# A new hand-written order of 1,343 operations in a fused hash-attention and channel-mix kernel

## The chip, the cores and the metric

The kernel runs on one core of one Trainium2 chip. The metric is the device time of one launch in microseconds; three runs of the kernel before gave a median of 245.75 us (245.43 to 245.88). Five engines work beside each other, each through its own instruction stream in order: PE (matrix multiplications), DVE (VectorE), ACT (ScalarE), POOL (GpSimd) and SP, which here only issues DMA transfers.

## The reference

Two stages are computed. The first is attention in which a query sees only the keys of its own hash bucket: six random projections give six sign bits for each query and key, and scores between different buckets are masked out before the softmax. The second is a channel mix over the attention's output.

```python
q_bits = (np.einsum('bhsd,dk->bhsk', q, proj) > 0).astype(np.int64)
k_bits = (np.einsum('bhsd,dk->bhsk', k, proj) > 0).astype(np.int64)
...
mask = q_bucket[:, :, :, None] == k_bucket[:, :, None, :]
scores = scale * np.matmul(q, k.transpose(0, 1, 3, 2))
scores = np.where(mask, scores, -1000000000.0)
...
attn = attn / (np.sum(attn, axis=-1, keepdims=True) + 1e-09)
return np.matmul(attn, v).astype(np.float32)
...
xk = mu_k * x + (1.0 - mu_k) * x_prev
xr = mu_r * x + (1.0 - mu_r) * x_prev
k = np.maximum(xk @ w_k, 0.0)
v = k * k @ w_v
r = 1.0 / (1.0 + np.exp(-(xr @ w_r)))
return (r * v).astype(np.float32)
```

The sizes are 4 batches, 8 heads, 768 positions and 64 values per head; the channel mix has width 512 and an inner width of 1,024. Inputs and output are float32.

## The kernel before

Two heads of one batch make a pair; there are 16 pairs, numbered 0 to 15, and four of them make a batch. For pair n the operations are, by the names that the code gives them:

- `ldq`, `ldv` (lines 360 and 365): loads of q, k and v, issued by SP. `wl` are loads of the weights.
- `hi`, `lo` (lines 265 and 431, on DVE from pair 2 on): q and k split into two 16-bit halves, high and low. `tr` (line 435): a DMA transpose of the split tensor into the tile `a`, issued by SP. Pairs 2 and 3 do this for q and k apart, later pairs in one piece. Pairs 0 and 1 are transposed on PE, with copies `evt` out of PSUM (line 259).
- `bits` (line 455, PE): the six projections; `bx` (line 458, DVE): their signs out of PSUM; `row` (line 259, POOL or DVE): four copies of the signs into rows of `a`, one for each of q and k of each head (`row1q1` is pair 1, q, second head). With those rows a matching bucket adds a large number to the score, which is how the mask is made.
- `sc` n_0 to n_8 (line 633, PE): the scores in nine steps of 1,024 columns; `exp` (line 637, ACT): their exponentials into the tile `pt`.
- `oo` n_0 and n_1 (line 660, PE): scores times v, three pieces for each head; `rc` and `ob` (lines 671 to 678, DVE): division by the row sums.
- `ot` with `xt`, or `otd` (lines 688, 694): the output transposed, on PE or by a DMA; `xs`, `df`, `xk`, `xr` (lines 701 to 733, DVE): the shifted mix, the inputs of the second stage.
- `va`, `mc` (lines 410 and 417, DVE) with `mean` (PE) and `vsum` (POOL): v less its mean.

After each fourth pair come the operations of the channel mix of that batch: `kp` (line 748, PE) with `relu` (line 754, ACT) and `sq` (line 759, DVE), `r` (line 772, PE) with `tanh` (line 775, ACT), and `v` (line 785, PE) with `os` (line 792, DVE) and the store `st` (line 795). They are spread among the attention of later pairs.

Nothing of this is ordered by the place in the source. Each `plan.add` only appends an operation to a list, with its reads and writes. The list `ORDER` then says in which order the operations are emitted, and each engine runs its own operations in that order. `BANKS` says which PSUM bank each result takes, or for `sc` and `bits` which pair of banks; a result that takes a bank waits until the operation that frees the bank's last content has run. `ENGS` says on which engine an operation runs where there is a choice. The waits between engines are put in from what is read and written, so every order that respects the data is correct; but an engine that has come to an operation whose input isn't there stands, with all that is behind it.

The score buffers `a` are 4 deep, `nat` (loads of q and k) 3, `nh` (the split) 2, `pt` 2.

Of the kernel before, what the change touches and what calls it, by code (L numbers as in the profile page):

```python
# [103 lines left out]
class Plan:  # L104
# [10 lines left out]
    def add(self, eng, dur, fn, r=(), w=(), take=None, give=(), name="", at=0.0, svc=0.0, tr=0, port=0, alts=()):  # L115
        o = Op()
        o.alts = alts
        if alts:
            e = ENGS[self.flex] if ENGS else eng
            self.flex += 1  # L120
            fn = lambda f=fn, e=e: f(e)
# [748 lines left out]
```

## Time and profile before

| | us |
|---|---|
| median of three runs | 245.75 |
| the profiled execution | 245.72 |
| its span, first to last instruction | 243.7 |
| PE busy, 2,466 matmuls | 231.5 |
| DVE busy, 407 instructions | 195.0 |
| ACT busy, 247 instructions | 185.2 |
| POOL busy, 140 instructions | 90.5 |

The span is 2.0 us shorter than the time of the execution it was taken from. In the timelines a row gives the start of a stretch of like instructions, its length, the engine and line, what it writes and reads, how many instructions it holds, and in brackets the idle time of the engine ahead of it with what ended it. In the windows a row gives, for a stretch of time, its length and the busy time and instructions of PE, of PE's weight loads, of DVE, ACT and POOL, then the granted clock of PE, the share of the DMA engines and the rate.

### The profile page before, as it was taken

Reading aid. Unit: us, or ns where it says so; the run is one execution under the profiler, and the core shown is the slowest. Engines: PE = TensorE matmul, PEld = TensorE weight load, DVE = VectorE, ACT = ScalarE, POOL = GpSimd, SP = SyncE. Lnnn points to the kernel's source line nnn. Section 1 sums busy time; section 2 is a strip of 40 time slices with the busy share of each in tenths; the row PEclk is TensorE's granted clock in tenths of the full one; section 3 lists DMA queues with packets and bytes.
Section 4 is the critical chain, followed back from the end, with each engine's and each line's share of the span. In section 5 each row is a group of like instructions: output and inputs, shape, how many; then the busy total and the mean of one; then the engine's idle time right before and its main releaser. Section 6 shows DMA issues by size and latency. Waiting matters only on the chain.

```text
span 243.7 us, 6161 instructions
## 1 busy us (share of the span) xinstructions
PE 231.5 (95%) x2466; PEld 143.1 (59%) x2486; DVE 195.0 (80%) x407; ACT 185.2 (76%) x247; POOL 90.5 (37%) x140
## 2 busy tenths in 40 slices
PE   8998899998989999999999999999999999999994
PEld 6654566675656656565658565556565764555443
DVE  3998899999999999899989999956556779636342
ACT  3999999998988889888889948898987860145420
POOL 5691756797755966505225260105020000000000
PEclk9999999999999999999999999999999999999999
DMA  6989999999999899999999929149302030222033
GB/s 227 377 238 194 216 238 212 310 222 377 280 241 225 287 236 258 233 255 240 261 222 251 181 62 175 54 107 208 118 3 58 9 116 5 87 86 89 0 129 129
DMA packets 72523, 43.97 MB, mean 180 GB/s; under 512 B 54832, under 2 KB 67504, under 8 KB 72496
## 3 DMA queue, kind: packets, MB, share of 16 engines
q1 hardware_dynamic: 72272, 43.40, 73.2%
q8 instruction: 19, 0.31, 0.5%
q10 hardware_dynamic: 224, 0.20, 0.2%
q14 instruction: 8, 0.07, 0.1%
HBM read 24.12 MB, written 6.29 MB: 125 GB/s over the span
## 4 chain that ended last, share of the span: by engine, by line
PE 60%; DVE 23%; DMA 7%; ACT 4%; issue 4%; SPq 1%; DVEq 0%; ACTq 0%
PE ps_all L785 17%; PE ps_all L633 12%; PE ps_all L748 11%; PE ps_all L772 8%; PE ps_all L660 7%; DMA a<-nh 5%; DVE nh L431 4%; DVE nh L265 3%; DVE k L759 3%; ACT pt L637 3%; DVE bx L458 3%; DVE a L259 2%; PE ps_all L455 2%; DMA mur<-in_moe_mu_r_dram 2%; PE ps_all L282 2%
## 5 line engine op out<-in xcount | busy, mean ns | idle before, releaser
L637 ACT ACTIVATE pt<-ps_all 128x1024 bf16<-128x1024 f32 x144 | 139.7, 1043 | 13.4 <-PE ps_all L633 12.0
L633 PE MATMUL ps_all<-a 128*128 128x512 f16 (+1 forms) x384 | 81.2, 325 | 3.0 <-ACT pt L637 0.9
L259 POOL COPY a<-bx 6x384 f32<-6x384 f32 x46 | 34.8, 756 | 54.3 <-DVE bx L458 18.1
L660 PEld LDWEIGHTS <-pt 128*128 128x128 bf16 x1152 | 43.9, 97 | 10.7 <-issue 1.1
L748 PE MATMUL ps_all<-xk,wk 128*128 128x384 bf16 x256 | 48.6, 326 | 1.1 <-DVE ob L678 1.1
L633 PEld LDWEIGHTS <-a 128*128 128x128 f16 x384 | 33.3, 97 | 25.6 <-issue 5.3
L660 PE MATMUL ps_all<-va,pt 128*128 128x65 bf16 x1152 | 46.4, 193 | 0.0
L785 PE MATMUL ps_all<-wv,k 128*128 128x512 bf16 (+2 forms) x200 | 45.3, 362 | 0.3
L754 ACT ACTIVATE kr<-ps_all 128x384 bf16<-128x384 f32 x64 | 29.7, 507 | 20.9 <-PE ps_all L748 16.2
L759 DVE TENSOR_TENSOR k<-kr 128x384 bf16<-128x384 bf16 x64 | 25.0, 414 | 13.5 <-ACT kr L754 13.1
L748 PEld LDWEIGHTS <-wk 128*128 128x128 bf16 x256 | 24.0, 98 | 17.0 <-issue 1.7
L785 PEld LDWEIGHTS <-k 128*128 128x128 bf16 x208 | 19.5, 98 | 19.4
L431 DVE SCALAR_TENSOR_TENSOR nh<-nat,nh 128x1536 f16<-128x1536 f32 (+1 forms) x16 | 27.9, 1744 | 0.2
L792 DVE SCALAR_TENSOR_TENSOR os<-rs,ps_all 128x512 f32<-128x512 f32 (+2 forms) x26 | 16.6, 643 | 13.2 <-PE ps_all L785 8.8
L775 ACT ACTIVATE rs<-ps_all 128x512 f32<-128x512 f32 x24 | 14.3, 600 | 15.0 <-DVE os L792 8.5
L772 PE MATMUL ps_all<-wr,xr 128*128 128x512 bf16 x84 | 23.3, 379 | 0.8 <-issue 0.2
L386 POOL TENSOR_TENSOR vt<-vn 128x384 f32<-128x384 f32 x12 | 13.8, 1148 | 20.0 <-DMA vn<-in_v_dram 19.6
L678 DVE TENSOR_TENSOR ob<-ps_all,rc 128x384 bf16<-128x384 f32 x32 | 17.7, 554 | 0.7
L265 DVE TENSOR_SCALAR nh<-nat 128x1536 f16<-128x1536 f32 (+2 forms) x21 | 16.8, 809 | 0.7 <-DMA nat<-in_k_dram 0.5
L458 DVE TENSOR_SCALAR bx<-ps_all 128x768 uint16<-128x768 uint16 x15 | 14.2, 954 | 2.8 <-ACT pt L637 2.3
L410 DVE SCALAR_TENSOR_TENSOR va<-ps_all,vn 128x384 bf16<-128x384 f32 x24 | 12.7, 548 | 2.9 <-PE ps_all L405 2.9
L772 PEld LDWEIGHTS <-xr 128*128 128x128 bf16 x96 | 9.0, 97 | 9.4 <-issue 0.5
(94 smaller groups left out, 190.1 us busy)
## 6 DMA issues: line engine op xcount, KB each, us to landing
vn<-in_v_dram SPq DMA_DIRECT2D x16, 384.0 KB, 4.9
out_dram<-os SPq DMA_DIRECT2D x23, 256.0 KB, 2.3
nat<-in_q_dram SPq DMA_DIRECT2D x15, 384.0 KB, 5.2
nat<-in_k_dram SPq DMA_DIRECT2D x15, 384.0 KB, 5.7
wst<-in_moe_w_k_dram SPq DMA_DIRECT2D x2, 512.0 KB, 7.7
wst<-in_moe_w_r_dram SPq DMA_DIRECT2D x2, 512.0 KB, 7.6
wst<-in_moe_w_v_dram SPq DMA_DIRECT2D x2, 512.0 KB, 6.2
k<-in_moe_w_k_dram SPq DMA_DIRECT2D x1, 512.0 KB, 6.5
```

Source lines behind the costliest of these rows:

```text
L259: nc.scalar.copy(o, i_) if e == "ACT" else tt_on(e).tensor_copy(o, i_)
L265: tt_on(e).tensor_scalar(out=o, in0=i_, scalar1=QS, scalar2=None, op0=ALU.mult)
L431: nc.vector.scalar_tensor_tensor(out=nh[:, :, D:P], in0=nat.rearrange("p j (c d) -> p (j c) d", d=D), scalar=QS, in1=nh[:, :, 0:D], op0=AL ...
L458: nc.vector.tensor_scalar(out=bx_t[sx][0:rows].bitcast(U16), in0=ps_t[plan.slot[nm]][0:rows, 0:S].bitcast(U16).rearrange("p (c e) -> p c e ...
L633: nc.tensor.matmul(ps[:, lo - s * STEP : hi - s * STEP], side_a["k"][sa][:, j, jc * P : (jc + 1) * P], side_a["q"][sa][:, j, q0 : q0 + hi ...
L637: nc.scalar.activation(out=pt_t[sp][:, s * STEP : (s + 1) * STEP], in_=ps_t[plan.slot[nm]], func=AF.Exp, bias=EBIAS, scale=ESC)
L660: nc.tensor.matmul(oo[:, ic * 65 : ic * 65 + 65], pt_t[sp][:, o : o + P], va_t[sa][:, j, jc, 0 : D + 1], start=(not uc and ic == 0 and jc ...
L748: nc.tensor.matmul(ps[:, 0:HALF], wk_sb[:, d, fc * P : (fc + 1) * P], xk_t[mx[d]][:, h * HALF : (h + 1) * HALF], start=(d == 0), stop=(d = ...
L754: nc.scalar.activation(out=kr_t[sk], in_=i_, func=AF.Relu, scale=0.5 ** 0.5)
L759: nc.vector.tensor_tensor(out=k2_t[s2][:, h * HALF : (h + 1) * HALF], in0=kr_t[sk], in1=kr_t[sk], op=ALU.mult)
L772: nc.tensor.matmul(sm(nr), xr_t[mx[d]][:, c * P : (c + 1) * P], wr_sb[:, d, :], start=(d == 0), stop=(d == NDC - 1))
L785: nc.tensor.matmul(sm(nv)[:, x0:x1], k2_t[(b * NFC + fc) % NK2][:, c * P : (c + 1) * P], wv_sb[:, fc, x0:x1], start=(fc == 0), stop=(fc == ...
```

## The change

`ORDER` and `BANKS` are replaced; `ENGS` and every operation stay. Of the operations on each engine, counted by their place in that engine's own sequence, these have another one than before: PE 366 of 466 (the first at its 48th), DVE 312 of 383 (from its 26th), ACT 182 of 247 (from its 27th), POOL 76 of 133 (from its 35th), SP none of 114. 225 of the 337 names of PSUM results are in another bank. In `Plan.add`, three lines are added, which put the duration and port of the chosen engine into the plan's record.

```diff
-    73, 78, 1, 75, 26, 27, 33, 34, 35, 30, 31, 76, 74, 79, 28, 29, 32, 40, 118, 77, 119, 80, 120, 41, 42, 43, 44, 45, 46, 47, 48, 84, 85,
...
-    139, 189, 190, 117, 140, 49, 23, 24, 153, 148, 25, 149, 191, 192, 152, 154, 141, 155, 142, 159, 150, 241, 157, 144, 143, 193, 160, 146,
-    165, 163, 156, 242, 158, 145, 166, 164, 161, 167, 168, 169, 244, 245, 216, 217, 204, 205, 235, 210, 212, 243, 246, 194, 162, 195, 211,
...
+    73, 1, 27, 33, 34, 35, 0, 2, 3, 4, 5, 6, 7, 8, 9, 10, 37, 36, 38, 39, 78, 76, 74, 75, 82, 83, 125, 79, 118, 77, 133, 126, 111, 119, 30,
...
+    154, 25, 191, 140, 149, 141, 155, 159, 192, 241, 142, 146, 242, 244, 144, 150, 160, 156, 157, 158, 165, 166, 163, 164, 216, 161, 245,
+    143, 145, 204, 217, 205, 162, 190, 49, 193, 235, 243, 194, 246, 288, 287, 51, 183, 170, 50, 212, 167, 294, 208, 195, 213, 171, 210, 295,
...
         if alts:
             e = ENGS[self.flex] if ENGS else eng
             self.flex += 1
+            for a in alts:
+                if a[0] == e and e != eng: dur, port = a[1], a[2]
+            eng = e
             fn = lambda f=fn, e=e: f(e)
```

Read by names (the number in `ORDER` in brackets), these stretches of single engines are those that the prediction speaks of. The first is DVE from its 23rd operation on:

```
before: evt1k0(132) evt1q1(136) lo2(189) evt1k1(140) hi2(191) lo2(192) bx1(142) hi3(241) row1q1(144) row1q0(143) row1k1(146)
        lo3(242) row1k0(145) rc0(168) ob0(169) hi3(244) lo3(245) bx2(195)
after:  evt1k0(132) evt1q1(136) lo2(189) hi2(191) evt1k1(140) lo2(192) hi3(241) bx1(142) row1k1(146) lo3(242) hi3(244)
        row1q1(144) lo3(245) row1q0(143) row1k0(145) muk(50) hi4(294) bx2(195)
```

PE, from its 42nd, and POOL, from its 35th:

```
PE before:   sc0_1 bits1 sc0_4 sc0_6 sc0_5 oo0_0 sc0_8 oo0_0 sc0_7 oo0_0 sc1_8 sc1_2 sc1_5 sc1_6 bits2 sc1_4
PE after:    sc0_1 bits1 sc0_4 sc0_6 sc0_5 oo0_0 oo0_0 sc0_8 sc1_8 sc0_7 sc1_2 bits2 oo0_1 sc1_6 oo0_0 sc1_4
POOL before: va2 vsum2 vsum2b row2k0 row2q0 row2k1 row2q1 vsum2c row3k1 row3q1 row3k0 row3q0
POOL after:  row2q1 row2q0 row2k0 va2 row2k1 vsum2 vsum2b row3q1 row3k0 row3k1 row3q0 vsum2c
```

On ACT `exp1_8 exp1_2 exp0_7` follow each other before and after. Next, DVE from its 49th and PE around `bits4`:

```
DVE before: lo5 va3 rc1 ob1 rc1 ob1 muk xs0 bx4 df0 xr0 xt1 hi6 xk0 lo6 rc2 rc2 ob2 xs1 ob2 bx5
DVE after:  mur lo5 xs0 va3 df0 xr0 rc1 ob1 rc1 ob1 bx4 hi6 xt1 lo6 rc2 rc2 xs1 ob2 ob2 df1 bx5
PE before:  oo1_1 sc2_5 bits4 sc3_0 sc3_3 sc3_6 ot1 sc3_5 oo2_0 sc2_8
PE after:   oo1_0 sc2_5 sc3_8 sc3_0 bits4 sc3_3 oo2_0 sc3_5 oo2_0 ot1
```

After the change `sc3_0` takes the two banks that the two `ob1` free. Further on, `bits6` stands ahead of `sc5_7` before and behind it after. Last, DVE from about its 101st and PE around `bits7`:

```
DVE before: sq0_2 hi8 sq0_3 lo8 rc5 ob5 sq0_2 sq0_4 sq0_3 xr2 sq0_6 bx7
DVE after:  sq0_1 hi8 xz5 xr3 sq0_2 lo8 bx7 rc5 sq0_3 ob5
PE before:  sc6_8 kp0_6_0 sc6_5 bits7 kp0_5_1 kp0_6_0 sc6_1
PE after:   sc6_8 bits7 kp0_3_1 kp0_6_0 sc6_5 kp0_4_1 oo5_0 sc6_1
```

There `kp0_5_1` takes the bank that the first `ob5` frees before the change, and `sc6_1` takes the banks that `bx7` frees after it. Up to `sc6_1`, PE has run the same operations in both but for these: the kernel before has eight more `kp` matmuls ahead of it (both parts of `kp0_4_0`, the first of `kp0_5_1`, the last of `kp0_6_0`), the kernel after three `kp` matmuls (the first part of `kp0_4_1`) and twelve of `oo5_0`.

114 rows, old and new, of tables (BANKS, ORDER) are left out of this document.

## The prediction

> **What bounds the kernel now.** I read the page first, then windows of 10 us, then who waited for whom, then timelines of single engines.
>
> ```profile
> span 243.7 us, 6161 instructions
> ...
> PE   8998899998989999999999999999999999999994
> ...
> DVE  3998899999999999899989999956556779636342
> ...
> DMA  6989999999999899999999929149302030222033
> ```
>
> ```profile
> 20.00:30.00 10.00, 8.16 (x101) 4.60 (x98) 8.41 (x13) 9.62 (x11) 4.41 (x5) 1.00 0.91 207
> 30.00:40.00 10.00, 9.65 (x141) 6.52 (x139) 9.47 (x16) 10.00 (x12) 5.91 (x10) 1.00 1.18 250
> 40.00:50.00 10.00, 9.57 (x170) 6.76 (x167) 9.93 (x16) 9.72 (x11) 7.68 (x10) 1.00 0.99 270
> 50.00:60.00 10.00, 9.05 (x142) 6.31 (x141) 9.67 (x18) 9.07 (x11) 8.57 (x8) 1.00 1.12 285
> 60.00:70.00 10.00, 10.00 (x104) 6.55 (x103) 9.42 (x17) 10.00 (x17) 8.52 (x10) 1.00 1.12 261
> 70.00:80.00 10.00, 8.90 (x107) 5.72 (x106) 9.59 (x22) 8.02 (x13) 4.26 (x7) 1.00 1.26 228
> 80.00:90.00 10.00, 9.62 (x114) 5.77 (x115) 9.90 (x19) 8.41 (x12) 7.61 (x7) 1.00 1.18 317
> 140.00:150.00 10.00, 9.44 (x120) 6.07 (x114) 9.76 (x23) 6.80 (x10) 4.09 (x4) 1.00 0.56 118
> ```
>
> The granted clock (the column after POOL's) is 1.00 throughout, so the time is PE's work plus the holes in it. PE works without a break in the second half; its holes lie in these eight windows and sum to 1.84 + 0.35 + 0.43 + 0.95 + 0.00 + 1.10 + 0.38 + 0.56 = 5.6 us. That is all a new order can win after 20 us. In the same windows up to 90 us DVE is busy 9.4 to 9.9 of 10 us from 30 us on and ACT nearly as much, so a hole of PE is there mostly the shadow of a full DVE or ACT, or of a transfer:
>
> ```profile
> PEld L455 <- DMA a<-nh: 2.4, 4, 1.0
> ...
> PE ps_all L748 <- DVE ob L678: 1.1, 1, 1.1
> ```
>
> **The change part by part.** The three lines in Plan.add touch a record that schedule doesn't read, and SP's order stays: both cost nothing. The rest is order. I follow the places where an operation now stands behind another.
>
> First stretch, from 14.6 us:
>
> ```profile
> 15.07 0.74 DVE L265 TENSOR_SCALAR nh<-nat 128x768 f16<-128x768 f32 x1
> ...
> 18.39 1.76 DVE L259 COPY a<-bx 6x384 f32<-6x384 f32 x3
> 20.18 0.96 DVE L431 SCALAR_TENSOR_TENSOR nh<-nat,nh 128x768 f16<-128x768 f32 x1
> 21.17 0.35 DVE L259 COPY a<-bx 6x384 f32<-6x384 f32 x1
> ...
> 22.25 0.55 DVE L265 TENSOR_SCALAR nh<-nat 128x768 f16<-128x768 f32 x1
> 22.84 0.96 DVE L431 SCALAR_TENSOR_TENSOR nh<-nat,nh 128x768 f16<-128x768 f32 x1
> ```
>
> ```profile
> 21.57 1.48 PE L633 MATMUL ps_all<-a 128*128 128x256 f16 x9 [0.76 <-DVE a L259]
> ```
>
> ```profile
> 22.22 23.96 ACT L637 ACTIVATE pt<-ps_all 128x1024 bf16<-128x1024 f32 x26 [0.35 <-PE ps_all L633]
> 46.35 10.41 ACT L637 ACTIVATE pt<-ps_all 128x1024 bf16<-128x1024 f32 x11 [0.17 <-PE ps_all L633]
> 57.69 4.69 ACT L637 ACTIVATE pt<-ps_all 128x1024 bf16<-128x1024 f32 x5 [0.93 <-PE ps_all L633]
> ```
>
> ```profile
> L259 DVE COPY a<-bx x14: 351/362/894, 18.4 to 183.3; 6x384 f32<-6x384 f32 x14
> ```
>
> ```profile
> 18.03 1.05 POOL L386 TENSOR_TENSOR vt<-va 128x390 f32<-128x390 bf16 x1
> ```
>
> hi2 now runs ahead of evt1k1, which bits1 waits for: that is up to 0.74 us on bits1, sc0_4 and sc0_6 and the exponentials behind them. It does not add to what follows, since the next wait of ACT ends later. sc1_2 waits for row1k0, the copy at 21.17, and PE (hole of 0.76) and ACT (0.35) stood for it already. In the new order a second hi3 and lo3 (0.55 + 0.96) run ahead of it, so it ends 1.51 us later. From this comes off what the copies gain: the dearest of the 14 took 0.894, the median 0.362, and the three at 18.39 sum to 1.76; while they ran, POOL ran vsum2 (the 1.05 row), which now stands behind the row copies of pair 2. If row1q1 falls to the median, 0.53 comes off. So exp1_2 starts between 0.98 and 1.51 us later; I take 1.0, since POOL has nothing to run there. exp0_7 stands behind exp1_2 and cannot fill the gap. ACT then goes without a break for 23.96 us, 26 exponentials of 0.92 each, so this 1.0 is kept until its next hole.
>
> On the shared port, the Trainium skill (SBUF — State Buffer, Who interferes with whom) says that a VectorE instruction in a two-port mode and a GpSimd instruction block each other for a whole instruction, whoever issues first. By that rule the copy falls to 0.36 and the delay is 0.98; by the row alone, if 0.89 is what a first copy costs, it is 1.51. The trace agrees as far as it goes: the dear copy is the one that ran beside POOL.
>
> The same move makes both lo3 earlier. Ahead of the first, two of the three copies go (1.76 less one of 0.36, so 1.4 us); the second then follows it by one hi3 and one copy, and starts at 20.7 to 21.2 in place of 22.84. With them go the transposes of pair 3, whose first SP issued right after lo3 (20.18 + 0.96):
>
> ```profile
> 21.16 4.09 SPq L435 DMA_TRANSPOSE a<-nh  x2
> ```
>
> ```profile
> 44.94 0.83 PE L455 MATMUL ps_all<-a,p 128*32 128x512 f16 x16 [0.43 <-DMA a<-nh]
> ```
>
> The DMA engines are full from there (share 0.91 to 1.26), so whatever is queued behind, the transposes of pairs 4 to 6 too, may land 1.4 to 2 us earlier. What this can win is the 2.4 us in which PE waited for a transpose, at bits5 for one (the second row), and ACT's holes of 0.17 and 0.93. I count none of it in the sum: ACT's 1.0 us at 22 us takes up ACT's two holes, and the next stretch takes the transposes off PE's path.
>
> POOL: va2, vsum2 and vsum2b (0.8 to 1.05 each) move from a hole of POOL to behind row copies. Their first reader is oo2_0, which PE reaches after bits4 in both orders (36.32 before); that hides them.
>
> Second stretch:
>
> ```profile
> 36.50 0.56 DVE L678 TENSOR_TENSOR ob<-ps_all,rc 128x384 bf16<-128x384 f32 x1
> ...
> 37.30 0.96 DVE L458 TENSOR_SCALAR bx<-ps_all 128x768 uint16<-128x768 uint16 x1
> ...
> 38.76 1.14 DVE L724 SCALAR_TENSOR_TENSOR xr<-df,mur,xt 128x768 bf16<-128x768 bf16 x1
> ```
>
> ```profile
> 36.32 0.83 PE L455 MATMUL ps_all<-a,p 128*32 128x512 f16 x16
> 37.14 0.59 PE L633 MATMUL ps_all<-a 128*128 128x512 f16 x3
> ```
>
> Before, bits4 ran while DVE did ob1, and bx4 followed ob1 at once. Now sc3_0 needs the banks that ob1 frees, bits4 stands behind sc3_0, and bx4 right behind ob1 on DVE. DVE therefore stands from the end of ob1 for sc3_0 (0.43 to 0.59; the lower figure is the distance to the next start in a full pipe) and bits4 (0.83): 1.3 us, with hi6, xt1, lo6 and all else behind it. xt1 then waits for ot1, which PE has put behind oo2_0 and sc3_5, and these wait for exp3_0 and bx4: between 0 and 0.9 us more, I take 0.3. Against this, hi5 no longer waits long for its load: DVE may be 0.6 us earlier at lo5. Together DVE is 1.0 us behind when lo6 is done (0.7 to 1.9). In the windows from 40 to 70 us DVE had 0.07 + 0.33 + 0.58 us idle; it can make up at most that, and I let it make up 0.6. It arrives at 70 us 0.4 us late.
>
> Third stretch:
>
> ```profile
> 68.94 0.56 DVE L759 TENSOR_TENSOR k<-kr 128x384 bf16<-128x384 bf16 x1
> 69.43 2.56 DVE L431 SCALAR_TENSOR_TENSOR nh<-nat,nh 128x1536 f16<-128x1536 f32 x1
> ...
> 74.80 0.95 DVE L458 TENSOR_SCALAR bx<-ps_all 128x768 uint16<-128x768 uint16 x1
> ```
>
> ```profile
> 72.93 0.81 PE L748 MATMUL ps_all<-xk,wk 128*128 128x384 bf16 x4 [1.10 <-DVE ob L678]
> 73.58 0.59 PE L633 MATMUL ps_all<-a 128*128 128x512 f16 x2
> ```
>
> PE's largest hole, 1.10 us, was for a bank that ob5 freed behind lo8. The new order takes that wait away and puts another in the same place: sc6_1 needs the banks of bx7, and bx7 stands behind hi8, xr3 and lo8. Before, lo8 ended at 71.99. Ahead of it xr3 now comes in (1.14, by the xr above) and sq0_3 goes out (0.56), so lo8 ends at 72.6 and bx7 at 73.6; with DVE's 0.4 us, at 74.0. sc6_1 thus starts 0.4 us later than the 73.58 of before. And by then PE has done less: eight kp matmuls out, three and twelve oo matmuls in.
>
> ```profile
> 75.35 0.74 PE ps_all L660 x24
> ...
> 218.77 5.20 PE ps_all L748 x32
> ```
>
> At 0.163 each the eight are 1.30 us; three with twelve of 0.031 are 0.86: 0.44 us less. PE is 0.4 + 0.4 = 0.8 us behind. After that PE has work of the channel mix in store; its holes of 0.38 and 0.56 in the windows at 80 and 140 us may go or come, and I set them equal. Sum: 245.72 + 0.8 = 246.5 us, from the profiled execution, whose time is 0.03 from the median.
>
> **The rivals.** (a) The landings decide: one mechanism, the earlier lo3. If the transposes of pairs 4, 5 and 6 land 1.5 us earlier, the 2.4 us of PE's waits for them go, and DVE, whose bx4 to bx6 hang on them, is early and not late, at 70 us too. Less the 1.0 us of ACT at 22 us that is 1.4: 244.3 us. It decides if the earlier landings reach bits5, which stood longest but one (44.94), before DVE's new stand at bx4 uses them up. For it: DMA shares above 1. Against: bits4 is now gated by ob1 and not by its landing.
>
> (b) Nothing is left of it: DVE makes up its delay in its 1.0 us of idle time from 40 to 70 us, and PE its 0.4 us of missing work in the window at 80 us. 245.7 us.
>
> (c) The delay isn't made up: DVE is 1.9 us behind at lo6 and, 9.4 to 9.9 full up to 90 us, stays so. PE then loses 1.9 at sc6_1, the missing 0.4, and once more a hole like that of the window at 140 us (0.56): 2.9 us, so 248.6 us.
>
> (d) That the change doesn't do what it says can be left out: each engine's sequence is fixed by the list.
>
> **How the numbers follow.** My forecast gets 0.42, (a) 0.31, (b) 0.14, (c) 0.13. About 0.2%, or 0.5 us, is what a measurement of this kernel can tell from no change. Faster by more is (a) with a little of the forecast's lower edge: 0.33. Within it lie (b) without its edges and nothing else: 0.13. Slower: 0.54. The forecast's own range is 245.9 to 247.5, from DVE's 0.7 and 1.9 at lo6. To hold 8 in 10 it must reach to (a) and most of (c): 243.9 to 248.9.
>
> **What would show each step.** At 22 us: an ACT hole of about 1.3 us ahead of the exponential that starts near 23.2, and a PE hole ended by a row copy. The split of pair 3 done by 21.7, and its transposes issued at once. At 38 to 40 us: DVE idle about 1.3 us, ended by PE L455. At 70 to 74 us: PE idle, ended by bx L458 in place of ob L678. If bits5 and bits6 have no wait for a DMA and DVE's bx6 comes before 57.2, (a) is right and I am wrong. If PE's holes between 90 and 160 us are well over the 0.6 of before, (c) is.

## The result, and the profile after

The changed kernel takes **248.72 us** (median of 6 runs, 248.04 to 249.39) beside 245.81 (6 runs, 245.11 to 246.36) of the kernel before: ratio **1.0123 [1.0097, 1.0148]**, 2.9 us slower. The forecast was 246.5, the range 243.9 to 248.9. The profiled execution is a late one: 249.31 us, span 247.1. Line numbers are three higher than before.

From the page: the span, the busy times, and the rows of PE and DVE in 40 slices of 6.2 us.

```profile
span 247.1 us, 6169 instructions
...
PE 233.2 (94%) x2469; PEld 142.7 (58%) x2486; DVE 194.7 (79%) x407; ACT 186.0 (75%) x247; POOL 87.7 (36%) x140
...
PE   7977999999999899999999899999999999999994
...
DVE  2998797999999998899989889995757494945242
```

PE's third and fourth slices (12 to 25 us) read 7 and 7, where before they read 9 and 8; DVE has two new dips to 7, at 25 to 31 and at 37 to 43 us. The windows of 10 us (columns as in the prediction: PE, PEld, DVE, ACT, POOL, clock, DMA share, GB/s):

```profile
20.00:30.00 10.00, 8.64 (x121) 5.20 (x123) 8.43 (x14) 9.47 (x11) 3.38 (x4) 1.00 1.05 233
30.00:40.00 10.00, 9.11 (x127) 5.90 (x123) 8.70 (x13) 10.00 (x12) 9.22 (x12) 1.00 1.14 255
40.00:50.00 10.00, 10.00 (x167) 6.63 (x168) 7.95 (x13) 9.58 (x11) 7.11 (x9) 1.00 1.17 277
...
70.00:80.00 10.00, 9.61 (x121) 6.12 (x119) 9.93 (x21) 8.11 (x12) 5.50 (x8) 1.00 1.10 252
80.00:90.00 10.00, 9.00 (x135) 6.17 (x136) 9.43 (x19) 9.31 (x13) 5.80 (x9) 1.00 1.11 298
...
130.00:140.00 10.00, 9.19 (x145) 6.70 (x145) 9.70 (x24) 8.32 (x10) 6.00 (x10) 1.00 0.71 173
```

DVE stands 2 us in the window at 40 us, and PE doesn't: it has no hole there at all. PE's holes are at 20 to 40, at 80 and, where it had none before, at 130 us. But windows at fixed times mix up what is done in them. So I also took PE's steps of each kernel in their order, counted each with its distance to the next in a full pipe, and read from the traces when a given amount of that work was done. The table says how many us each profiled execution was then behind the kernel before; e1 to e12 are the runs of the next section. The lag swings by up to 1 us where one order has passed a hole and the other has not, so the rows stand on level stretches of it.

```
time in the
kernel before   after   e1     e2     e6     e7     e8     e9     e12
 12.8 us        1.14  -0.13  -0.18   0.38   0.54   0.48   0.72  -0.16
 32.3           1.58   0.54   0.07   0.83   0.99   0.73   0.97   0.09
 42.0           2.61   0.54   0.97   1.81   2.06   2.55   1.88   1.11
 65.0           1.88   0.01   0.20   1.08   1.31   1.77   1.11   0.38
 76.3           1.17  -0.66  -0.51   0.37   0.61   1.07   0.25  -0.48
 87.1           2.11  -0.67   0.44   1.32   0.70   2.00   0.58  -0.16
132.5           2.39  -0.38   2.40   1.58   1.02   2.45   0.58  -0.13
137.5           3.42  -0.38   2.41   2.03   2.05   3.47   1.05   0.34
148.4           3.26  -0.32   2.66   1.39   1.90   3.31   0.40  -0.31
178.7           3.58  -0.31   2.64   2.43   2.22   3.63   1.44   0.56
```

The changed kernel was 1.14 us late already when its first score (sc0_0) was done. Of this, 0.77 us stands at the start of sc0_0 (13.05 us, before 12.28), and that is this execution's: with the same first operations e1, e2 and e12 started sc0_0 0.38 to 0.43 early, and e11, with the old ones, 0.83 late. It goes with the first small load, which DVE waited for 3.7 us here (2.8 before; view of the waits):

```profile
DVE pz L806 <- DMA pj<-in_proj_dram: 3.7, 1, 3.7
```

The rest comes inside sc0_0, and it belongs to the change, to `BANKS` and not to `ORDER`: t1k0 now lies in bank 5, one of the two that sc0_0 takes (before in bank 6), and sc0_0 stands for evt1k0, DVE's copy that frees it (PE after).

```profile
13.63 0.38 PE L636 MATMUL ps_all<-a 128*128 128x256 f16 x2 [0.20 <-DVE a L262]
```

sc0_0 takes 0.96 us here and 0.84 in the eight other executions that begin in the new order, but 0.60 in all five that begin in the old one.

From the row of 12.8 us on, what the change lost is 0.03 us up to 76 us, 0.94 from there to 87, 0.28 to 132, and 1.19 behind; with the 0.36 inside sc0_0 that is 2.8. From 179 us to the end nothing changes.

### The profile page after: what moved, and what is told of

Same layout as the page of the kernel before. It is cut to its first block, busy times and chain, and to the rows that moved or that the text cites. A ratio compares the mean times of both kernels' runs of the same rounds, so it can differ in the third digit from the quotient of the medians.

```text
span 247.1 us, 6169 instructions
## 1 busy us (share of the span) xinstructions
PE 233.2 (94%) x2469; PEld 142.7 (58%) x2486; DVE 194.7 (79%) x407; ACT 186.0 (75%) x247; POOL 87.7 (36%) x140
## 5 line engine op out<-in xcount | busy, mean ns | idle before, releaser
L636 PE MATMUL ps_all<-a 128*128 128x256 f16 (+1 forms) x384 | 81.8, 325 | 3.9 <-ACT pt L640 1.3
L262 POOL COPY a<-bx 6x384 f32<-6x384 f32 x46 | 33.7, 732 | 74.9 <-DVE bx L461 59.4
L663 PE MATMUL ps_all<-va,pt 128*128 128x65 bf16 x1152 | 45.5, 193 | 0.4 <-DVE va L413 0.4
L762 DVE TENSOR_TENSOR k<-kr 128x384 bf16<-128x384 bf16 x64 | 27.1, 439 | 11.6 <-ACT kr L757 11.5
L434 DVE SCALAR_TENSOR_TENSOR nh<-nat,nh 128x1536 f16<-128x1536 f32 (+1 forms) x16 | 26.6, 1660 | 0.2
L268 DVE TENSOR_SCALAR nh<-nat 128x1536 f16<-128x1536 f32 (+2 forms) x21 | 17.4, 838 | 1.1 <-issue 1.0
L389 POOL TENSOR_TENSOR vt<-vn 128x384 f32<-128x384 f32 x12 | 12.4, 1034 | 7.9 <-DMA vn<-in_v_dram 7.2
L458 PE MATMUL ps_all<-a,p 128*32 128x512 f16 (+1 forms) x240 | 12.3, 328 | 1.3 <-DVE a L262 1.0
```

Of the source, the lines that this page charges most:

```text
L262: nc.scalar.copy(o, i_) if e == "ACT" else tt_on(e).tensor_copy(o, i_)
L268: tt_on(e).tensor_scalar(out=o, in0=i_, scalar1=QS, scalar2=None, op0=ALU.mult)
L434: nc.vector.scalar_tensor_tensor(out=nh[:, :, D:P], in0=nat.rearrange("p j (c d) -> p (j c) d", d=D), scalar=QS, in1=nh[:, :, 0:D], op0=AL ...
L636: nc.tensor.matmul(ps[:, lo - s * STEP : hi - s * STEP], side_a["k"][sa][:, j, jc * P : (jc + 1) * P], side_a["q"][sa][:, j, q0 : q0 + hi ...
L663: nc.tensor.matmul(oo[:, ic * 65 : ic * 65 + 65], pt_t[sp][:, o : o + P], va_t[sa][:, j, jc, 0 : D + 1], start=(not uc and ic == 0 and jc ...
L762: nc.vector.tensor_tensor(out=k2_t[s2][:, h * HALF : (h + 1) * HALF], in0=kr_t[sk], in1=kr_t[sk], op=ALU.mult)
```

## The experiments

All have the changed kernel's text, `ORDER` and `BANKS` apart. Where two orders are joined, the banks of the second part are exchanged among each other so that nothing alive is overwritten.

| run | median us (range, runs) | kernel before | ratio [95%] |
|---|---|---|---|
| e1_new_to_30 | 245.80 (245.19 to 246.43, 12) | 245.69 | 1.0003 [0.9983, 1.0024] |
| e3_old_to_30 | 248.91 (248.76 to 249.91, 6) | 245.69 | 1.0148 [1.0123, 1.0173] |
| e2_new_to_121 | 248.34 (248.08 to 249.69, 6) | 245.69 | 1.0129 [1.0099, 1.0158] |
| e4_old_to_121 | 248.72 (247.51 to 249.26, 6) | 245.69 | 1.0128 [1.0100, 1.0156] |
| e5_relu_behind_exp | 248.14 (247.76 to 248.78, 6) | 245.55 | 1.0102 [1.0077, 1.0127] |
| e6_vsum12_later | 247.93 (247.39 to 248.52, 6) | 245.55 | 1.0088 [1.0064, 1.0111] |
| e7_ob6_ahead | 247.15 (246.40 to 248.34, 9) | 245.55 | 1.0062 [1.0040, 1.0084] |
| e8_hi6_ahead | 248.58 (247.93 to 249.34, 6) | 245.55 | 1.0117 [1.0093, 1.0141] |
| e9_new_mended | 247.02 (246.30 to 248.45, 12) | 245.77 | 1.0047 [1.0022, 1.0071] |
| e10_old_mended | 245.76 (244.37 to 247.11, 12) | 245.77 | 1.0002 [0.9978, 1.0026] |
| e11_old_ob5_ahead | 245.27 (244.85 to 246.54, 12) | 245.77 | 0.9992 [0.9972, 1.0012] |
| e12_new_mended_sq | 246.98 (246.17 to 248.44, 8) | 245.47 | 1.0063 [1.0039, 1.0087] |

### Half the order new, half old: four runs

```diff
-ORDER = new
+ORDER = first[:n] + [i for i in second if i not in first[:n]]
 # e1: new, old, n = 206   e3: old, new, 206
 # e2: new, old, n = 763   e4: old, new, 763
```

> The new order for the 206 operations that come first (up to about 30.7 us of PE, the first stretch), the old order for all others. Kernel before 245.8, changed kernel 248.7. Theory (the loss sits in two places: exchanges on DVE at 15 to 22 us that put sc0_4 to sc1_2 back, and one hole of PE at 135 us): PE was 2.1 us late at 19 us and 1.55 late at 26 us in the changed kernel, of which 0.77 was already there before the first score (first loads landing later, put down to that one execution); so +0.8 to +1.3 here: 246.6 to 247.1. Rival A (the earlier transposes give it back): 245.8 or less. Rival B (the loss comes from the second and third stretch, DVE 1.9 us behind at lo6): at most +0.4, 246.2. If the late start belongs to the order and not to the execution, the first loads land 0.8 us later here too and the sum is +2.0, 247.8.

> The old order for the first 206 operations, the new order for all others: the complement of the first run. Theory: 248.7 less what the first run lost, 247.4 to 247.9, with PE's hole of about 1 us at 135 us still there. Rival A: 248.7, as the first stretch cost nothing. Rival B: 248.3 or more. If the two halves of this pair do not add up to the 2.9 us, a delay made in the first stretch is made up or made worse by the rest.

> The new order for the first 763 operations (up to about 121 us of PE), the old order behind. Theory: all of the first place, none of the second: PE was 2.3 late at 102 to 132 us, less 0.77 of the start: +1.5, 247.3. Rival B (second and third stretch, growing): nearly all of the loss is here, 248.4 to 248.7. If the late stretch from 121 us on costs nothing by itself this equals the changed kernel; if it is the only cause this equals the kernel before.

> The old order for the first 763 operations, the new order behind: the complement of the second run. Theory: only the hole at 135 us and what follows it (PE's lag grew from 2.3 at 132 us to 3.2 to 3.6 behind it): +1.0 to +1.3, 246.8 to 247.1. Rival A and rival B: nothing is lost behind 121 us, 245.8. If ACT's relu1_3 again stands for DVE's sq1_1 while GpSimd runs vsum12, the hole is the order's own and not this execution's.

**The first stretch costs nothing** (e1: -0.4 to 0.6 us by the interval). Its complement e3 loses 3.2 us, up to 0.9 of them by a stand of ACT at its own joint, so at least 2.3. That is the size of rival A, and not of the theory. The timeline of ACT in e1 shows how:

```profile
16.91 2.85 ACT L640 ACTIVATE pt<-ps_all 128x1024 bf16<-128x1024 f32 x3 [0.36 <-PE ps_all L636]
20.05 1.95 ACT L640 ACTIVATE pt<-ps_all 128x1024 bf16<-128x1024 f32 x2 [0.28 <-PE ps_all L636]
22.70 3.83 ACT L640 ACTIVATE pt<-ps_all 128x1024 bf16<-128x1024 f32 x4 [0.71 <-PE ps_all L636]
...
50.07 10.43 ACT L640 ACTIVATE pt<-ps_all 128x1024 bf16<-128x1024 f32 x11 [0.27 <-PE ps_all L636]
```

ACT stands 1.35 us in three places where before it stood 0.35 in one: 1.0 more. But from 50.07 it then runs to 60.50 without a break, and the 0.93 us for which it stood before at 57.69 are gone. There ACT had waited for scores behind bits6, and bits6 for the transpose of pair 6. SP's rows for that transpose, first before, then e1:

```profile
44.78 7.76 SPq L435 DMA_TRANSPOSE a<-nh  x1
```

```profile
45.57 4.30 SPq L438 DMA_TRANSPOSE a<-nh  x1
```

Its issue took 4.30 us in place of 7.76, with the transposes ahead of it gone out earlier. It landed at 51.27, before at 56.17; those of pairs 4 and 5 landed at 34.25 and 41.37, before at 36.08 and 44.90. bits6 then starts at 56.18 without a wait; before it started at 56.22 after standing 0.71.

The pair cut at 121 us shows less than it was to: the joint makes a hole of its own in both, which neither whole kernel has (PE, e2 and e4):

```profile
122.28 0.81 PE L751 MATMUL ps_all<-xk,wk 128*128 128x384 bf16 x4 [1.14 <-DVE os L795]
```

```profile
122.59 0.81 PE L751 MATMUL ps_all<-xk,wk 128*128 128x384 bf16 x4 [0.90 <-ACT pt L640]
...
135.64 1.03 PE L636 MATMUL ps_all<-a 128*128 128x256 f16 x6 [0.81 <-ACT pt L640]
```

So the medians of e2 and e4 (2.65 and 3.03 over before) are each too high by the joint, 1.7 and 1.8 us by the count of the table. Without it, 1.0 us is lost up to 121 us and 1.2 behind. That takes the joints' size from the two profiled executions, and is an estimate. The last row is the changed kernel's hole at 135 us: it is the order's own, and comes with the old order in front too.

### The stall of DVE at 40 us filled: e8

```diff
 DVE:
-ob1, bx4, hi6, xt1, lo6
+ob1, hi6, bx4, lo6, xt1
```

> The changed kernel with the second stretch's stall of DVE filled: hi6 ahead of bx4 and lo6 ahead of xt1, so that DVE works in the 1.58 and 0.58 us in which it stood for bits4 and ot1. The prediction's fifth and sixth step and its rival with a DVE delay that is not made up say: DVE 1.4 us earlier from 45 us, and what of it reaches the banks of ob5 and ob6 is gained, 0.4 to 1.4: 247.3 to 248.3. Theory: nothing, since DVE stood 0.30 for PE at 57 us (rc4) and would only stand longer there; sc3_7 may wait 0.4 for xt1: 248.5 to 248.9.

This is the stall that the prediction's fifth step foretold, in the changed kernel (DVE) and in e8:

```profile
39.33 0.56 DVE L681 TENSOR_TENSOR ob<-ps_all,rc 128x384 bf16<-128x384 f32 x1
41.47 0.96 DVE L461 TENSOR_SCALAR bx<-ps_all 128x768 uint16<-128x768 uint16 x1 [1.58 <-PE ps_all L458]
...
43.88 0.56 DVE L262 COPY xt<-ps_all 128x768 bf16<-128x768 bf16 x1 [0.58 <-PE ps_all L691]
```

```profile
39.75 0.95 DVE L268 TENSOR_SCALAR nh<-nat 128x1536 f16<-128x1536 f32 x1
41.41 0.96 DVE L461 TENSOR_SCALAR bx<-ps_all 128x768 uint16<-128x768 uint16 x1 [0.71 <-PE ps_all L458]
42.28 1.75 DVE L434 SCALAR_TENSOR_TENSOR nh<-nat,nh 128x1536 f16<-128x1536 f32 x1
...
45.88 0.20 DVE L674 RECIPROCAL rc<-ps_all 128x6 f32<-128x6 f32 x1 [1.38 <-PE ps_all L663]
```

The 2.16 us of standing are still there, as 0.71 and 1.38 (and 0.17 more): DVE only stands for PE a few instructions later. Nothing is won (1.0117 beside 1.0123), as the theory said, though not at the place it named.

### The hole at 84 us: e7

PE, DVE and POOL of the changed kernel, from one timeline:

```profile
82.47 1.76 DVE L434 SCALAR_TENSOR_TENSOR nh<-nat,nh 128x1536 f16<-128x1536 f32 x1
...
82.98 2.15 POOL L262 CAST wv<-k 128x1024 bf16<-128x1024 f32 x1 [1.36 <-DMA k<-in_moe_w_v_dram]
...
84.15 1.19 DVE L762 TENSOR_TENSOR k<-kr 128x384 bf16<-128x384 bf16 x1
...
85.67 0.56 DVE L681 TENSOR_TENSOR ob<-ps_all,rc 128x384 bf16<-128x384 f32 x1
...
86.28 1.04 PE L775 MATMUL ps_all<-wr,xr 128*128 128x512 bf16 x3 [0.90 <-DVE ob L681]
```

r0_0 takes the bank that ob6 frees. Before, it took one that an exponential had freed. And ob6 stands behind lo9 and a squaring (sq0_4) that takes 1.19 us beside GpSimd's cast, where a free one takes 0.35.

```diff
 DVE:
-lo9, sq0_4, rc6, ob6
+lo9, rc6, ob6, sq0_4
```

> The changed kernel with rc6 and ob6 ahead of sq0_4 on DVE at 84 us. r0_0 waited for ob6's bank, PE stood 0.97 us. Theory (PE's late holes are the order of DVE between 66 and 88 us, where DVE never stands): ob6 ends about 1.1 earlier, the hole goes, relu0_6 keeps its time since sq0_4 then costs 0.35 and not 1.19 (GpSimd's wc6 has ended): 0.7 to 1.0 less, 247.7 to 248.0. Rival (the gain is given back, since DVE is the bound here and PE waits for it at the next bank): the hole comes back within 10 us, 248.5 to 248.7.

DVE and PE in e7:

```profile
83.99 0.56 DVE L681 TENSOR_TENSOR ob<-ps_all,rc 128x384 bf16<-128x384 f32 x1
84.46 0.88 DVE L762 TENSOR_TENSOR k<-kr 128x384 bf16<-128x384 bf16 x3
```

```profile
84.74 1.04 PE L775 MATMUL ps_all<-wr,xr 128*128 128x512 bf16 x4
```

The hole is gone, three squarings together cost 0.88, and the gain stays to the end of the trace. By the table it is 0.85 us between 76 and 87 us (0.09 lost there, not 0.94); the median says 1.6, and the intervals allow both. **This is the one mend that paid in full:** it doesn't only move a wait, it also takes 0.84 us of work off DVE (1.19 less 0.35).

### The hole at 135 us: e5 and e6

```profile
133.74 1.19 POOL L389 TENSOR_TENSOR vt<-vn 128x384 f32<-128x384 f32 x1
134.00 1.15 DVE L762 TENSOR_TENSOR k<-kr 128x384 bf16<-128x384 bf16 x1
...
135.18 0.49 ACT L757 ACTIVATE kr<-ps_all 128x384 bf16<-128x384 f32 x1 [1.33 <-DVE k L762]
...
136.64 1.03 PE L636 MATMUL ps_all<-a 128*128 128x256 f16 x6 [0.81 <-ACT pt L640]
```

Four engines in a chain (one timeline of the changed kernel): GpSimd's vsum12 holds up DVE's sq1_1, which reads the buffer that ACT's relu1_3 writes next; behind relu1_3 stands exp11_7, though its scores are there; and PE waits for exp11_7's bank. e5 undoes the order on ACT, e6 moves GpSimd's work (vsum13 has to follow vsum12).

```diff
 ACT, e5:
-relu1_3, exp11_7, exp11_6
+exp11_7, relu1_3, exp11_6
 POOL, e6:
-vsum12, vsum12b, vsum12c, row12k0, row13q0, vsum13, vsum13b, row13k1
+row12k0, row13q0, row13k1, vsum12, vsum12b, vsum12c, vsum13, vsum13b
```

> The changed kernel with one step of ScalarE undone: at 135 us relu1_3, which waits for DVE's sq1_1, goes behind exp11_7, whose scores have long been there. Changed kernel 248.7, kernel before 245.8. Theory (an order on ACT, not a full engine, makes the hole): sc11_8 no longer waits for exp11_7's bank; sc11_5 then waits for ob10 (136.42) and keeps about 0.35 of the 0.98, so 0.6 less and, if the lag of 142 us goes too, up to 1.0 less: 247.7 to 248.1. Rival (PE would have stood there anyway, behind DVE's ob10 and ob9): no gain, 248.7.

> The changed kernel with GpSimd's vsum12, vsum12b and vsum12c moved from 134 us behind row13k1 (146 us), where GpSimd has nothing to do; ACT and DVE keep their order. Theory (sq1_1 took 1.15 us because GpSimd worked beside it, 0.35 to 0.55 where it did not): sq1_1 ends 0.6 to 0.8 earlier, relu1_3, exp11_7 and ob10 too; the hole of 0.98 shrinks to 0.2 to 0.4: 248.0 to 248.2. Rival (sq1_1 is dear for another reason, or the wait moves to ob10): sq1_1 stays above 1 us, or the time stays at 248.7.

PE in e5; then, all of e6, one timeline of POOL, DVE and PE, ACT alone, and PE alone:

```profile
135.11 1.20 PE L636 MATMUL ps_all<-a 128*128 128x256 f16 x6
...
138.85 0.81 PE L751 MATMUL ps_all<-xk,wk 128*128 128x384 bf16 x4 [0.79 <-DVE ob L681]
```

```profile
132.92 0.71 POOL L262 COPY a<-bx 6x384 f32<-6x384 f32 x1
...
133.19 0.65 DVE L762 TENSOR_TENSOR k<-kr 128x384 bf16<-128x384 bf16 x1
...
135.33 1.03 PE L636 MATMUL ps_all<-a 128*128 128x256 f16 x6 [0.32 <-ACT pt L640]
```

```profile
150.31 0.49 ACT L757 ACTIVATE kr<-ps_all 128x384 bf16<-128x384 f32 x1 [1.18 <-DVE k L762]
```

```profile
151.76 1.08 PE L636 MATMUL ps_all<-a 128*128 128x512 f16 x5 [0.50 <-ACT pt L640]
```

e5: the hole of 0.81 goes, and 3.7 us later one of 0.79 stands at the next bank, ob9's. In its trace nothing is won (by the count of the table 1.22 us are lost behind 132 us, in the changed kernel 1.19), as its rival said. The median, 248.14, is 0.6 lower, next to the theory's 248.1; the two intervals overlap, so the times alone don't decide. e6: with sq1_1 at 0.65 the hole is 0.32, and from 132.5 to 148.4 us e6 gains 0.19 us on the kernel before, where the changed kernel loses 0.87. Then 0.7 goes at 151 us, to the same kind of chain: relu1_7 stands for a squaring that DVE has put behind lo14. Over all e6 loses 0.85 us behind 132 us in place of 1.19.

### Four mends together, and one more: e9 and e12

```diff
 DVE, e9 (with the edits of e6 and e7):
-sq0_0, va5, va5
+va5, va5, sq0_0
-va6, sq0_4, rc5, mc6, ob5
+sq0_4, rc5, ob5, va6, mc6
 DVE, e12 (on top of e9):
-lo14, sq1_5
+sq1_5, lo14
```

> The changed kernel with its four late stands mended together: va5 ahead of sq0_0 (66 us), sq0_4, rc5 and ob5 ahead of the second va6 (78 us), rc6 and ob6 ahead of sq0_4 (84 us), GpSimd's vsum12 from 134 to 146 us. Changed kernel 248.7, kernel before 245.8. Theory (the order of DVE behind 65 us makes the loss; the sizes by PE's holes): 0.53 + 0.55 + 0.97 + 0.5 = 2.5 less, 246.2, so most of the 2.9 us is found. Rival (DVE is full between 57 and 88 us, so a hole mended comes back at the next bank): only the 1.57 of rc6 and ob6 ahead remains, 247.1 or more.

> The mended changed kernel (247.0) with one more step of DVE exchanged: at 147 us the sq1_5 that ScalarE's relu1_7 waits for goes ahead of lo14 (1.75 us) and not behind it; its own input was there at 138 us. In the mended kernel ACT stood 1.19 us for it and PE 0.67 at sc12_1. Theory (what is left of the loss lies behind 121 us, in places where a squaring that frees ScalarE's buffer stands behind long work of DVE): PE's hole at sc12_1 goes, 0.5 to 0.7 less, 246.3 to 246.5, within 0.3 per cent of the kernel before. Rival (it comes back, as the hole of sc11_8 came back at ob9 when only ScalarE's order was changed): 246.9 to 247.1, with a new hole within 10 us.

e9 wins 1.7 us of the 2.9 and not 2.5. Beside e7 (247.15) the three other edits add nothing that can be told. One mend failed for a reason that the trace shows (DVE, POOL, PE in e9): sq0_4, put earlier, now collides with another cast, and the hole at sc6_0 that it was to close (0.39 in the changed kernel) is 0.45.

```profile
76.47 1.45 DVE L762 TENSOR_TENSOR k<-kr 128x384 bf16<-128x384 bf16 x2
```

```profile
76.51 1.20 POOL L262 CAST wr<-wst 128x1024 bf16<-128x1024 f32 x1
```

```profile
78.86 0.59 PE L636 MATMUL ps_all<-a 128*128 128x512 f16 x3 [0.45 <-DVE ob L681]
```

In e12 the hole at 151 us is gone, and the next one stands 3 us later, at a bank that DVE frees (PE): 246.98 beside 247.02. The rival holds.

```profile
153.83 1.03 PE L636 MATMUL ps_all<-a 128*128 128x256 f16 x6 [0.38 <-DVE os L795]
```

### The same mends in the kernel before: e10 and e11

```diff
 DVE, e11:
-lo8, rc5, ob5
+rc5, ob5, lo8
 PE and DVE, e10 (with the edit of e11):
-bits6, sc5_7
+sc5_7, bits6
-rc6, bx8, xz6, sq0_4
+bx8, sq0_4, rc6, xz6
```

> The kernel before with its own largest holes mended in the same manner: sc5_7 ahead of bits6 on PE (55 us), rc5 and ob5 ahead of lo8 on DVE (71 us), bx8 and sq0_4 ahead of rc6 on DVE (84 us). Kernel before 245.8. Theory (holes of PE behind 50 us are worth their size when a step of DVE's or PE's order makes them): up to 0.6 + 1.1 + 0.6 = 2.3 less, 243.5; 0.6 of it may be lost to ACT, which is full to 70 us: 243.5 to 244.5. Rival (DVE and ACT bound this stretch, a hole only moves): 245.3 to 245.8.

> The kernel before with rc5 and ob5 ahead of lo8 on DVE at 69 us, and nothing else: PE's hole of 1.10 us at kp0_5_1 goes. This is what the prediction's sixth step said the change would not win, because another wait takes its place. Theory: 0.7 to 1.1 less, 244.7 to 245.1. Rival (the wait moves to bx7, sc6_1 or tr8, which lo8 now makes 0.9 later): no gain, 245.6 to 245.9.

PE in e11:

```profile
75.04 0.53 PE L663 MATMUL ps_all<-va,pt 128*128 128x65 bf16 x12 [0.34 <-ACT kr L757]
...
85.55 0.59 PE L636 MATMUL ps_all<-a 128*128 128x512 f16 x3 [0.42 <-DVE bx L461]
```

PE's largest hole of before, 1.10 us at kp0_5_1, is gone. A part comes back 2 us later behind ACT (the first row), and another at 85 us behind DVE (0.18 there in the kernel before). The time can't be told from that of the kernel before, and with three holes mended (e10) neither.

## Why the prediction was right in sign and short in size

- **First stretch: right in size by luck, and rightly left out of the sum.** 1.0 us on ACT was foretold, 1.0 measured (e1). But exp1_2 has only 0.36 of it (0.71 for 0.35). The other 0.64 stands ahead of exp0_6 and exp0_8, pair 0's, where the prediction let the delay of bits1 add nothing. The four row copies on DVE took 0.35 to 0.36 each, as foretold. The delay went into ACT's later hole, as written, since bits6 no longer stands. The earlier transposes, which the prediction counted at nothing, made room for that: pair 6's was issued 0.79 us later in e1, and with the 11.4 us from issue to landing of before it would have landed at 56.96 by this estimate, and not at 51.27. They landed 1.8 to 4.9 us earlier, where 1.4 to 2 was foretold.
- **Second stretch: about right, and of no weight in the end.** DVE stands 1.58 us for bits4 (1.3 foretold) and 0.58 for ot1 (0.3). From 32 to 42 us PE falls 1.0 us further behind; by 65 us 0.7 of that is made up, and by 76 all. e8 shows that DVE, when the stall is filled, stands for PE instead.
- **Third stretch: the step that gave the sum its 0.8 us failed, by one term.** It said that sc6_1's wait for bx7 takes the place of the hole for ob5, with bx7 done at 74.0. For that it let lo8 keep the 2.56 us of before. But before, GpSimd's vsum7 ran beside lo8 (POOL before); in the changed kernel GpSimd does nothing then, and lo8 takes 1.75. First vsum7 before, then lo8, bx7, oo5_0 and sc6_1 in the changed kernel:

```profile
69.37 1.00 POOL L386 TENSOR_TENSOR vt<-vn 128x384 f32<-128x384 f32 x1
```

```profile
71.58 1.75 DVE L434 SCALAR_TENSOR_TENSOR nh<-nat,nh 128x1536 f16<-128x1536 f32 x1
73.25 0.94 DVE L461 TENSOR_SCALAR bx<-ps_all 128x768 uint16<-128x768 uint16 x1
...
73.94 0.53 PE L663 MATMUL ps_all<-va,pt 128*128 128x65 bf16 x12
...
74.31 0.59 PE L636 MATMUL ps_all<-a 128*128 128x512 f16 x2
```

  lo8 takes 2.55 to 2.56 us in the two traces with vsum7 beside it (before, e4), and 1.74 to 1.75 in the twelve others. So bx7 ends at 74.19, in an execution that began 1.14 late: 0.95 earlier than foretold, although DVE came to hi8 0.45 late, as foretold (0.4). PE doesn't stand for it: the new order has given it other matmuls up to sc6_1. Less the 1.14, sc6_1 starts at 73.17, 0.41 us earlier than before and not 0.4 later. Against that stand the 0.44 us of work that PE has done less, as counted. So at 76 us the change costs 0.03 us, not 0.8.
- **Where the loss is, the prediction looked away.** "Its holes ... may go or come, and I set them equal" was the step that mattered: 0.94 us come between 76 and 87 us and 1.19 behind 132. Both places show in the order itself: r0_0's bank now belongs to ob6, and relu1_3 stands ahead of exp11_7. The price comes from which squaring meets GpSimd: in these two places one does, and costs 1.15 to 1.19 us. The kernel before has three over 0.9 us, but elsewhere, and the prediction did not ask which ones the new order would put beside GpSimd. So the sign came right by another way than the one foretold.
- **Rival (a)** had its mechanism right and its price wrong: the landings came, and only paid back the first stretch. Half of its sign came too: in the changed kernel bits5 and bits6 don't wait for a transpose, but bx6 starts at 59.74 us and not before 57.2. **Rival (c)** named nearly the time, 248.6, for a reason that e8 speaks against: filling DVE's stall of 2.16 us wins nothing. Its sign, holes well over 0.6 us between 90 and 160 us, did come. The range was stretched to 248.9 to take in (c), so that the measured time lies in it is luck. **Rival (b)** is what holds to 76 us.

Shown by a run: e7's 0.85 us, e6's part of the hole at 135 us, that the first stretch costs nothing, and that filling the second one's stall wins nothing. Open: the 0.28 us between 87 and 132 us, and most of what is lost behind 132 (every mend there came back in part). Up to the start of sc0_0 the new order can't be told from the old: nine executions of it came there -0.43 to 0.77 us from the kernel before, four others of the old one -0.50 to 0.83.

## What to carry to other kernels

A hole of PE is not worth its size when the engine that ends it is nearly full: four of the holes mended here (e5, e6, e11, e12) came back, whole or in part, within 2 to 16 us. The one mend that paid in full also took work off that engine, by keeping a short VectorE instruction away from a long one of GpSimd; whether that is why it paid was not tried apart. The duration of an instruction is part of the order, too: lo8 fell from 2.56 to 1.75 us because nothing of GpSimd stood beside it any more. And a forecast for a new order has to be followed to the end of the kernel: look at each result whose bank or buffer is freed by another operation than before, in the late stretches too.

## What the runs showed of the hardware

A squaring on DVE (both inputs in SBUF, 0.35 us alone) that meets an instruction of GpSimd ends 0.21 to 0.22 us after it, whatever the other is: 85.34 after 85.13 (cast), 135.15 after 134.93 (f32 add), 133.84 after 133.63 (row copy, e6), 77.92 after 77.71 (cast, e9), all from the rows above. It is held for the rest of the other instruction, not slowed. GpSimd is held in turn: the cast at 82.98 took 2.15 us, 0.90 of it behind the end of lo9, where one of the same shape took 1.20 (e9). The fourteen traces together have 896 squarings. 161 of them take over 0.5 us, and each of these ends 0.20 to 0.22 us after a GpSimd instruction that began before it; the 621 that meet none take 0.32 to 0.36 us. The Trainium skill (SBUF — State Buffer, Who interferes with whom) says that a VectorE instruction with two inputs in SBUF contends with a GpSimd instruction that reads SBUF, and, of VectorE's two-port modes, that the side that comes second is blocked and not throttled. The trace agrees in these four pairs, where it is the squaring that came second.
